# The sums of batches three and four by way of DRAM, and a first block in halves

## The chip, the cores and the metric

The kernel runs on one core of a Trainium2 chip. The metric is the device time of one execution in microseconds; a kernel's time is the median over several executions. The engines are named as the profile names them: PE (TensorE, matrix products), PEld (its weight loads), DVE (VectorE), ACT (ScalarE), POOL (GpSimd) and SP (SyncE, which here only issues transfers). Every engine works through its own list of instructions in order.

## The reference

A polynomial-sketch attention feeds a feed-forward layer. There are 4 batches, 4 heads, 1088 positions and 32 values per head; the sketch has r = 8, so a feature vector has 64 entries. All inputs and the output are float32.

```python
a = einsum('rd,bhsd->bhsr', S1, x);  b = einsum('rd,bhsd->bhsr', S2, x)
phi(x) = einsum('bhsi,bhsj->bhsij', a, b).reshape(..., 64)

kv  = einsum('bhsf,bhsd->bhfd', phi(k), v)      # sums of values, 64 x 32 a head
z   = sum(phi(k), axis=2)                       # own sums, 64 a head
num = einsum('bhsf,bhfd->bhsd', phi(q), kv)
den = einsum('bhsf,bhf->bhs', phi(q), z) + 1e-06
x   = (num / den), heads side by side           # 4352 x 128
out = maximum(x @ w_in, 0)**2 @ w_out           # w_in 128 x 2048, w_out 2048 x 128
```

## The kernel before

**The feed-forward layer as a stream of blocks.** The 4352 rows are cut into eight chunks of 512 (two of each batch, `ci = 2 * b + g`) and a ninth of 256 for the remainders. A chunk takes 16 blocks, one for each 128 columns of `w_in`. In a block PE multiplies `xT` (float16, rows along the free axis) by 128 columns of `w_in` into `pg` (L949), DVE or ACT takes the maximum with zero into `gt`, ACT or POOL squares it into `g`, and PE adds the product with 128 rows of `w_out` to `po` (L1037, float32, in two passes, hence "x2" in the profile). `block()` first calls `first_product()` until the stream holds more than `LOOK` = 3 finished first products, then takes the oldest for the second product. `now[0]` counts the blocks that were written out. After each block `pump` lets a number of generators ("lanes") write out some of the remaining work, so the order on every engine is fixed when the kernel is built; `dve_time`, `pool_time`, `quiet` and the like are the writer's guesses of how busy an engine is, used only for that.

**The attention of a batch** (`batch_gen`, for batches 1 to 3; batch 0 is written out by hand at the start). Blocks of `k` and `q` are turned by DVE, projected (L269, L288), and copied by ACT (L292, L294). The features of `q` are made by POOL (L338) from two factors, `f[0]` and `f[1]`, which `factors_gen` spreads over the partitions by way of DRAM: for each group `g` of a batch one transfer `q_one` and two `q_two` out (L311, L316), and two transfers `f` back (L325, L328). All of these are issued by SP, group 0 first and group 1 six blocks later. The features of `k` are made by POOL as outer products (L356).

`KvRows.products` then has PE form the sums of values, `kvr_ps` (L439; four heads of 32 rows each, 64 features along the free axis), and the own sums (L394). ACT copies both to SBUF (L458, L462). `spread` puts them into the block-diagonal matrix `kvbd[b]`, which has 128 partitions (two heads of 64 features) and, for two pairs of heads, 33 columns a head: 32 sums of values and the own sum. For that PE turns the sums of values with the identity (`turn`, L480) and picks the own sums with a 0/1 matrix (`pick_sums`, L406) into `kvt_ps`; ACT copies the values into place (`place`, L488), and DVE masks and adds up the own sums (`own_sums`, L414, L421).

Only then can `x_gen` write out the numerators and denominators of 512 rows (`nd`, L269, PE). `normalize` divides and scales on DVE and gives `xs`, whose turned form is the chunk's `xT`. There are two ways for that. If at the time of writing fewer than 15 blocks are left before the chunk's own first block (L626, `16 * chunk - now[0] < 15`), PE turns it with four transposes into `x_ps` (L631) and ACT copies it (L636). Otherwise DVE turns blocks of 32 (`xsT`, L648) and five transfers put them in place by way of DRAM (L650, L656). `second_gen` does the features and `x_gen` of a batch's second group, after the first group's chunk is there.

A finished chunk's `po` is turned by DVE (L917), scaled on POOL (L922) and stored by four transfers (L929). The scales go to all partitions by two small transfers (`beta`, L670, L671).

**SP's queue.** SP issues nearly all transfers in the order in which they were written out. An issue waits when its source is not ready, and everything behind it waits too.

**The start.** Batch 0 is written out by hand (L1046 to L1146). While the first rows are normalised, PE does products whose results nobody reads (`idle_products`). `first_two` then does the first products of blocks 0 and 1 at once: DVE and ACT each take one maximum, ACT and POOL one square each. The last two of four casts of `w_in` to float16 (L1143) follow on ACT before the stream begins. `later` lists loads by the block before which they are written out.

Of the kernel before, what the change touches and what calls it, by code (L numbers as in the profile page):

```python
# [21 lines left out]
def kernel(  # L22
# [17 lines left out]
    nc = tc.nc  # L40
# [198 lines left out]

    def idle_products(n, slow=False):  # L240
        idle_ps = pspool.tile([128, 512], F32, name="idle_ps", tag="po", bufs=2)
        for i in range(n):
            if slow:
                nc.tensor.matmul(idle_ps[:, :], zero_w[:, :], _v(zero_w, 0, [[0, 512]]))  # L244
            else:
                nc.tensor.matmul(idle_ps[:, :], zero[:, 0:128], zero[:, :])  # L246
# [181 lines left out]
    class KvRows:  # L428
# [34 lines left out]

        def products(self, phs):
            for g in range(2):
# [8 lines left out]
            self.rest_sums()  # L474
            self.keep_rows()
            self.keep_sums()

# [8 lines left out]
        def place(self, t_ps):  # L486
            for x in range(2):
                act.copy(  # L488
                    _v(kvbd[self.b], VW * x, [[2 * VW, 2], [1, D]], 64 * x, 64),
                    _v(t_ps, 0, [[D, 2], [1, D]], 64 * x, 64),  # L490
                )

        def spread(self):
# [268 lines left out]
    def batch_gen(b):  # L762
# [49 lines left out]
        kv = KvRows(b, ab_k)  # L812
        kv.products(phk)
        yield 1, 0
        nd_taken[0] = False
        yield from ms_both()
        ms_used()
        t_ps = kv.spread()
        yield 1, 0
        yield from dve_ready(1.0)  # L820
        own_sums(b, t_ps, 64)
        dve_time(0.6)
        lanes.append([second_gen(b, fs, w, phT, n1), n1 + 10, 0])
        yield 1, 0
        while not made_ph[b]:
# [3 lines left out]
    def second_gen(b, fs, w, phT, n1):  # L829
# [4 lines left out]
        for g in range(2):  # L834
            if w[g] > 512:
                u = b - 1 + g
                phT_rem[u] = [phT[g][pr][:, 512:576] for pr in range(2)]
                rests.append(u)
        yield 1, 0
        yield from x_gen(b, 1, phT[1], rests)  # L840
        if b % 2 == 1:
# [131 lines left out]

    def first_two():
        xT = chunks[0][0]
        pgs, gts, g2s = [], [], []
        for c in range(2):
            pgs.append(pspool.tile([128, 512], F32, name="pg", tag="pg", bufs=2))
            nc.tensor.matmul(pgs[c][:, :], w_in[:, 128 * c : 128 * c + 128], xT[:, :])
            gts.append(fpool.tile([128, 512], F32, name="gt", tag="gt", bufs=3))  # L980
            g2s.append(fpool.tile([128, 512], F32, name="g2", tag="g2", bufs=4))
        dve.tensor_scalar(
            out=gts[0][:, :], in0=pgs[0][:, :], scalar1=0.0, scalar2=None, op0=amax
        )
        act.activation(gts[1][:, :], pgs[1][:, :], Relu)
        act.activation(g2s[0][:, :], gts[0][:, :], Square)
        pool.tensor_tensor(out=g2s[1][:, :], in0=gts[1][:, :], in1=gts[1][:, :], op=mult)
        for c in range(2):
            stream.append((0, c, 512, g2s[c]))
            made[0] += 1  # L990

# [24 lines left out]
    def block():  # L1016
        while len(stream) <= LOOK and first_product():
            pass
# [4 lines left out]
        if nt < 512:  # L1023
# [7 lines left out]
            if c == NC - 1:  # L1031
                rows_store(0, ci)
                for args in held:
                    rows_product(*args)
                rows_store(1, ci)
            return
        nc.tensor.matmul(  # L1037
# [42 lines left out]
    outer(phq, pq[1], 0, 2, dve, pq[0])  # L1080
    outer(phq, pq[1], 3, 1, pool)
    for t in range(4):
        kv0.tile(phk[0], 0, t)
    zt_ps = pspool.tile([128, 32], F32, name="zt_ps", tag="po", bufs=2)
    pick_sums(zt_ps, 0, kv0.sums)
    outer(phq, pq[1], 2, 1, dve, pq[0])
# [5 lines left out]

    def turned_half(ph, t0, engs):
        t_ps = pspool.tile([128, 512], F32, name="t_ps", tag="ms", bufs=2)
        for pr in range(2):
            for t in (t0, t0 + 1):
                nc.tensor.transpose(  # L1097
                    _v(t_ps, 256 * pr + 128 * (t - t0), [[1, 128]]),
                    ph[:, 256 * t + 128 * pr : 256 * t + 128 * pr + 128],
                    iden[:, :],  # L1100
                )
        halves = []
# [26 lines left out]
    beta = next(norm)  # L1129
    idle_products(2)  # L1130
    chunk_of(0, 0, xT0, beta)
    for b in range(1, B):
        pool.memset(kvbd[b][:], 0.0)
        clear_rest(b)
    first_two()
    pq1 = proj(xq1, "ms")
    phq1 = ph_tile("ph_q", 2)
    for t0 in (0, 2):
        outer(phq1, pq1[1], t0, 2, pool)
    for _ in range(2):  # L1140
        first_product()
    for c in range(2, 4):
        act.copy(  # L1143
            w_in[:, 512 * c : 512 * c + 512], w_in32[:, 512 * c : 512 * c + 512]
        )
    nd_taken[0] = True  # L1146
# [15 lines left out]
    add_work(*(batch_gen(b) for b in range(1, B)))  # L1162
    later = []
    for b in range(2, B):
# [3 lines left out]
        later.append((n + 5, load_all, (q_sb[b], q, b)))  # L1168
        later += [(n + 6 + i, load_v_rest, (b, i, sp)) for i in range(2)]
    while len(stream) or made[0] < NC * (2 * B + 1):  # L1170
        while later and later[0][0] <= now[0]:
# [38 lines left out]
```

## Time and profile before

| What | Value |
|---|---|
| Median of 3 runs | 195.78 us (195.59 to 196.67) |
| Profiled execution, its own time | 195.83 us |
| Its span, first to last instruction | 194.0 us |
| PE, DVE, ACT, POOL busy | 186.3, 116.7, 109.2, 73.4 us |
| Second products L1037, x256 | 130.7 us |
| First products L949, x126 | 47.8 us |
| Features of `q` on POOL, L338 x12 | 16.1 us, idle before them 11.6 us for `f` |
| Idle products L246, x12 | 4.7 us |
| Transfers on SP's queue | 34400 packets, 22.27 MB |
| Mean granted clock of PE | 0.995 |

The span is that of one profiled execution, so sums of its parts are set against 194.0 us; some 1.8 us of the measured time lie outside it. Products are pipelined and overlap in the profile, so the chain that ended last, which counts every moment once, is a better price list for PE than mean durations. "Idle before, and what ended it" tells which other engine or transfer released an instruction. A row of SP is the time that the issue took, not the transfer itself.

### The profile page before, as it was taken

How to read it: one execution, taken by the hardware profiler on the slowest of the kernel's cores; microseconds unless marked ns; L12 is line 12 of the kernel's file. 1: busy time of each engine (PE TensorE's matmuls, PEld its weight loads, DVE VectorE, ACT ScalarE, POOL GpSimd, SP SyncE). 2: the span in 40 equal slices, each digit the busy share in tenths (PEclk: the TensorE clock that was granted, in tenths of full speed). 3: DMA queues.
4: the chain of work that ended last, by engine and by line, in shares of the span. 5: the costliest groups of instructions: out<-in, count | busy, mean ns of one | idle time of the engine just before them, and what ended most of it. 6: DMA issues, size and time to landing. Idle time of an engine off the chain costs nothing.

```text
span 194.0 us, 3759 instructions
## 1 busy us (share of the span) xinstructions
PE 186.3 (96%) x1390; PEld 97.0 (50%) x1390; DVE 116.7 (60%) x268; ACT 109.2 (56%) x215; POOL 73.4 (38%) x100
## 2 busy tenths in 40 slices
PE   7699999999999999999999999999899999999992
PEld 2573554545545454635454545454544344444791
DVE  4866785465477639376867264584477645544771
ACT  3254757654565964654847564557464665465470
POOL 4507502565247029251733280726124222522200
PEclk9999999999999999999999999999999999999998
DMA  5999674398953808974000467396011400300031
GB/s 160 268 314 228 159 216 132 66 234 203 233 203 93 198 4 198 275 219 84 4 3 0 81 164 199 80 222 144 3 25 33 63 7 0 54 0 0 9 51 27
DMA packets 34658, 22.58 MB, mean 116 GB/s; under 512 B 24720, under 2 KB 30096, under 8 KB 34640
## 3 DMA queue, kind: packets, MB, share of 16 engines
q1 hardware_dynamic: 34400, 22.27, 46.5%
q8 instruction: 11, 0.18, 0.4%
q10 hardware_dynamic: 240, 0.07, 0.2%
q14 instruction: 7, 0.06, 0.1%
HBM read 15.97 MB, written 6.37 MB: 115 GB/s over the span
## 4 chain that ended last, share of the span: by engine, by line
PE 85%; DVE 3%; issue 2%; DMA 2%; POOL 2%; SPq 2%; ACT 1%; POOLq 0%
PE po L1037 51%; PE pg L949 15%; PE nd L269 5%; PE kvr_ps L439 2%; DMA v_sb<-in_v_dram 2%; PE po L996 2%; PE po_r L996 2%; PE ab_ps L269 2%; POOL phF L338 1%; DVE gt L966 1%; PE ab_ps L288 1%; PE t_ps L1097 1%; PE idle_ps L244 1%; SPq L119 1%; PE kvt_ps L480 1%
## 5 line engine op out<-in xcount | busy, mean ns | idle before, releaser
L1037 PE MATMUL po<-g,w_o 128*128 128x512 f32 x256 | 130.7, 592 | 0.1
L966 DVE TENSOR_SCALAR gt<-pg 128x512 f32<-128x512 f32 (+1 forms) x105 | 67.7, 647 | 57.7 <-PE pg L949 49.9
L969 ACT ACTIVATE g<-gt 128x512 f32<-128x512 f32 (+1 forms) x105 | 62.6, 597 | 58.6 <-DVE gt L966 55.5
L1037 PEld LDWEIGHTS po<-g,w_o 128*128 128x128 f32 x256 | 48.5, 191 | 38.5 <-issue 20.1
L957 POOL TENSOR_TENSOR g<-gt 128x512 f32<-128x512 f32 x22 | 22.9, 1039 | 69.6 <-ACT gt L956 69.6
L949 PE MATMUL pg<-xT,w_in 128*128 128x512 f16 x126 | 47.8, 380 | 0.2 <-DVE gt L966 0.2
L949 PEld LDWEIGHTS <-w_in 128*128 128x128 f16 x142 | 13.8, 98 | 26.3 <-issue 25.3
L338 POOL TENSOR_TENSOR phF<-f,f 128x576 f32<-128x576 f32 (+1 forms) x12 | 16.1, 1361 | 11.6 <-DMA f<-q_two 11.6
L356 POOL TENSOR_TENSOR ph_k<-ab 128x512 f32<-128x512 f32 x14 | 14.5, 1070 | 10.4 <-ACT ab L294 9.0
L956 ACT ACTIVATE gt<-pg 128x512 f32<-128x512 f32 x22 | 12.8, 582 | 0.1
L922 POOL TENSOR_TENSOR o_sb<-oT,beta_t 128x512 f32<-128x512 f32 x8 | 8.4, 1048 | 5.2 <-DVE oT L917 4.9
L963 ACT ACTIVATE g<-gt 128x512 f32<-128x512 f32 x15 | 9.4, 629 | 0.6
L269 PEld LDWEIGHTS nd<-kvbd,phF 128*64 128x64 f32 x208 | 6.9, 137 | 5.3 <-issue 3.0
L962 ACT ACTIVATE gt<-pg 128x512 f32<-128x512 f32 x15 | 8.8, 585 | 0.0
L269 PE MATMUL nd<-kvbd,phF 128*64 128x66 f32 x208 | 7.9, 225 | 0.6 <-POOL phF L338 0.6
L917 DVE STREAM_TRANSPOSE oT<-po 128x512 f32<-128x512 f32 x8 | 5.7, 717 | 3.8 <-PE po L1037 3.5
L269 PEld LDWEIGHTS ab_ps<-w_bd,xt 128*64 128x64 f32 x160 | 6.1, 138 | 3.5 <-issue 1.4
L269 PE MATMUL ab_ps<-w_bd,xt 128*64 128x64 f32 x160 | 6.3, 224 | 1.1 <-DVE xt L257 1.1
L996 PE MATMUL po<-w_o,g 128*128 128x128 f32 x32 | 6.2, 278 | 0.0
L257 DVE STREAM_TRANSPOSE xt<-q_sb 128x512 f32<-128x512 f32 x8 | 5.4, 696 | 1.2 <-DMA q_sb<-in_q_dram 1.1
L996 PE MATMUL po_r<-w_o,g 128*128 128x128 f32 x32 | 6.0, 275 | 0.0
L246 PE MATMUL idle_ps<-zero 128*128 128x512 f16 x12 | 4.7, 522 | 1.3 <-DVE own L193 1.2
(131 smaller groups left out, 139.2 us busy)
## 6 DMA issues: line engine op xcount, KB each, us to landing
q_two<-qf SPq DMA_DIRECT2D x8, 288.0 KB
f<-q_one SPq DMA_DIRECT2D x4, 576.0 KB
f<-q_two SPq DMA_DIRECT2D x4, 576.0 KB
v_sb<-in_v_dram SPq DMA_DIRECT2D x16, 128.0 KB
out_dram<-o_sb SPq DMA_DIRECT2D x32, 64.0 KB
k_sb<-in_k_dram SPq DMA_DIRECT2D x3, 544.0 KB
q_sb<-in_q_dram SPq DMA_DIRECT2D x3, 544.0 KB
w_in<-in_moe_w_in_dram SPq DMA_DIRECT2D x2, 512.0 KB
```

What stands on the lines that cost most here:

```text
L269: nc.tensor.matmul(out_ps[p0 + c : p0 + c + z, c0 : c0 + w], lhsT[:, l0 + c : l0 + c + z], rhs)
L338: pool.tensor_tensor(out=ph[:, c], in0=fs[g][0][:, c], in1=fs[g][1][:, c], op=mult)
L356: eng.tensor_tensor(out=_v(ph, 256 * t0, [[64, 4 * m], [8, 8], [1, 8]]), in0=_v(ab if a is None else a, c0, [[n, 4 * m], [1, 8], [0, 8]]), ...
L949: nc.tensor.matmul(pg[:, 0:nt], w_in[:, 128 * c : 128 * c + 128], xT[:, 0:nt])
L956: act.activation(gt[:, 0:nt], pg[:, 0:nt], Relu)
L957: pool.tensor_tensor(out=g2[:, 0:nt], in0=gt[:, 0:nt], in1=gt[:, 0:nt], op=mult)
L962: act.activation(gt[:, 0:nt], pg[:, 0:nt], Relu)
L963: act.activation(g2[:, 0:nt], gt[:, 0:nt], Square)
L966: dve.tensor_scalar(out=gt[:, 0:nt], in0=pg[:, 0:nt], scalar1=0.0, scalar2=None, op0=amax)
L969: act.activation(g2[:, 0:nt], gt[:, 0:nt], Square)
L996: nc.tensor.matmul(po[r][:, 0:128], g2[:, 128 * r : 128 * r + 128], w_o[:, 128 * c : 128 * c + 128], start=c == 0, stop=c == NC - 1,)
L1037: nc.tensor.matmul(po[0][:, 0:nt], w_o[:, 128 * c : 128 * c + 128], g2[:, 0:nt], start=(c == 0), stop=(c == NC - 1),)
```

## The change

It has four parts.

1. For batches 2 and 3 (the third and fourth), `spread` and `own_sums` are replaced by `by_dram`. ACT copies the own sums and DVE turns the sums of values in blocks of 32 x 32, both into one tile `kept`. SP writes them to DRAM in two transfers and reads them back in eight: two of `kvbd` and two of `zs` for each half of the partitions. DVE adds up the four candidates of each own sum straight into `kvbd`. `second_gen` is added as a lane before that instead of after it, and now waits for POOL's counter before its `x_gen`. Batch 1 stays with `spread`.
2. The first block is done in two halves of 256 rows (`in_halves`), the first on DVE alone, the second on ACT alone; its second product has two halves too. The first blocks look ahead by `now[0] + 1` instead of 3.
3. At the start `pick_sums` comes before the first sums of rows, one idle product of two goes, and the casts of the second half of `w_in` are written out after blocks 3 and 6.
4. `turned_half` gets an argument `z` that nobody sets.

As L626 depends on the block counter, the way in which a chunk is turned can change with it.

```diff
...
@@ -461,7 +461,7 @@
             self.sums = apool.tile([128, 32], F32, name="kvz", tag="kvz")
             act.copy(self.sums[:, :], self.sums_ps[:, 0:32])
 
-        def products(self, phs):
+        def products(self, phs, keep=True):
             for g in range(2):
                 for t in range(4):
                     self.tile(phs[g], g, t)
@@ -472,8 +472,9 @@
                         self.sums_ps, self.abs, 128 * g + 32 * t, 256, t, g == 0, g == 1 and t > 0
                     )
             self.rest_sums()
-            self.keep_rows()
-            self.keep_sums()
+            if keep:
+                self.keep_rows()
+                self.keep_sums()
 
         def turn(self, t_ps):
             for x in range(2):
@@ -489,6 +490,54 @@
                     _v(kvbd[self.b], VW * x, [[2 * VW, 2], [1, D]], 64 * x, 64),
                     _v(t_ps, 0, [[D, 2], [1, D]], 64 * x, 64),
                 )
+
+        def by_dram(self):
+
+
+            b = self.b
+            kept = apool.tile([128, 96], F32, name="kept", tag="kept")
+            act.copy(kept[:, 64:96], self.sums_ps[:, 0:32])
+            dve.transpose(kept[:, 0:64], self.ps[:, 0:64])
+            parts = dpool.tile([128, 64], F32, name=f"kept{b}", tag=f"kept{b}")
+
+            kz = dpool.tile([32, 128], F32, name=f"keptz{b}", tag=f"keptz{b}")
+            sp.dma_start(parts[:, :], kept[:, 0:64])
+            sp.dma_start(
+                bass.AP(kz.tensor, kz.offset, [[8, 128], [1024, 4], [1, 8]]),
+                _v(kept, 64, [[8, 4], [1, 8]]),
+            )
+            yield 3, 0
+            zs = apool.tile([128, 8], F32, name="zs", tag="zs")
+            for x in range(2):
+                for i in range(2):
+                    sp.dma_start(
+                        _v(
+                            kvbd[b], VW * x, [[2 * VW, 2], [1, D]], 64 * x + 32 * i, 32
+                        ),
+                        bass.AP(
+                            parts.tensor, parts.offset + 32 * 64 * x + 32 * i,
+                            [[64, 32], [64 * 64, 2], [1, 32]],
+                        ),
+                    )
+                for pr in range(2):
+                    sp.dma_start(
+                        _v(zs, 4 * pr, [[1, 4]], 64 * x, 64),
+                        bass.AP(
+                            kz.tensor, kz.offset + (1024 + 64) * (2 * pr + x),
+                            [[1, 64], [256, 4]],
+                        ),
+                    )
+                yield 1, 0
+            yield 2, 0
+            yield from dve_ready(1.0)
+            for x in range(2):
+                dve.tensor_reduce(
+                    out=_v(kvbd[b], VW * x + D, [[2 * VW, 2]], 64 * x, 64),
+                    in_=_v(zs, 0, [[4, 2], [1, 4]], 64 * x, 64),
+                    axis=AX,
+                    op=add,
+                )
+            dve_time(0.4)
 
         def spread(self):
             t_ps = pspool.tile([128, 512], F32, name="kvt_ps", tag="ms", bufs=2)
@@ -810,17 +859,26 @@
             yield 1, 0
         yield from take_nd()
         kv = KvRows(b, ab_k)
-        kv.products(phk)
-        yield 1, 0
-        nd_taken[0] = False
-        yield from ms_both()
-        ms_used()
-        t_ps = kv.spread()
-        yield 1, 0
-        yield from dve_ready(1.0)
-        own_sums(b, t_ps, 64)
-        dve_time(0.6)
+        if b > 1:
+            yield from dve_ready(1.0)
+        kv.products(phk, b == 1)
         lanes.append([second_gen(b, fs, w, phT, n1), n1 + 10, 0])
+        if b == 1:
+            yield 1, 0
+            nd_taken[0] = False
+            yield from ms_both()
+            ms_used()
+            t_ps = kv.spread()
+            yield 1, 0
+            yield from dve_ready(1.0)
+            own_sums(b, t_ps, 64)
+            dve_time(0.6)
+        else:
+            moved = kv.by_dram()
+            dve_time(0.4)
+            yield next(moved)
+            nd_taken[0] = False
+            yield from moved
         yield 1, 0
         while not made_ph[b]:
             yield 1, 0
@@ -836,7 +894,10 @@
                 u = b - 1 + g
                 phT_rem[u] = [phT[g][pr][:, 512:576] for pr in range(2)]
                 rests.append(u)
+        ready = pool_free[0]
         yield 1, 0
+        while now[0] < ready and not hurry[0]:
+            yield 1, 0
         yield from x_gen(b, 1, phT[1], rests)
         if b % 2 == 1:
             add_work(rest_x(b // 2))
@@ -971,23 +1032,31 @@
         made[0] += 1
         return True
 
-    def first_two():
+    def half(t, i):
+
+        return _v(t, 64 * i, [[128, 4], [1, 64]])
+
+    def in_halves(c):
+
         xT = chunks[0][0]
-        pgs, gts, g2s = [], [], []
-        for c in range(2):
-            pgs.append(pspool.tile([128, 512], F32, name="pg", tag="pg", bufs=2))
-            nc.tensor.matmul(pgs[c][:, :], w_in[:, 128 * c : 128 * c + 128], xT[:, :])
-            gts.append(fpool.tile([128, 512], F32, name="gt", tag="gt", bufs=3))
-            g2s.append(fpool.tile([128, 512], F32, name="g2", tag="g2", bufs=4))
+        pgs, gts, g2s = [
+            [tl.tile([128, 512], F32, name=n, tag=n, bufs=bufs) for i in range(2)]
+            for tl, n, bufs in ((pspool, "pg", 2), (fpool, "gt", 3), (fpool, "g2", 4))
+        ]
+        for i in range(2):
+            nc.tensor.matmul(
+                pgs[i][:, 0:256], w_in[:, 128 * c : 128 * c + 128], half(xT, i)
+            )
         dve.tensor_scalar(
-            out=gts[0][:, :], in0=pgs[0][:, :], scalar1=0.0, scalar2=None, op0=amax
-        )
-        act.activation(gts[1][:, :], pgs[1][:, :], Relu)
-        act.activation(g2s[0][:, :], gts[0][:, :], Square)
-        pool.tensor_tensor(out=g2s[1][:, :], in0=gts[1][:, :], in1=gts[1][:, :], op=mult)
-        for c in range(2):
-            stream.append((0, c, 512, g2s[c]))
-            made[0] += 1
+            out=gts[0][:, 0:256], in0=pgs[0][:, 0:256], scalar1=0.0, scalar2=None, op0=amax
+        )
+        act.activation(gts[1][:, 0:256], pgs[1][:, 0:256], Relu)
+        dve.tensor_tensor(
+            out=g2s[0][:, 0:256], in0=gts[0][:, 0:256], in1=gts[0][:, 0:256], op=mult
+        )
+        act.activation(g2s[1][:, 0:256], gts[1][:, 0:256], Square)
+        stream.append((0, c, 512, g2s))
+        made[0] += 1
 
     po = [None, None]
     held = []
@@ -1014,7 +1083,7 @@
             (sp, act)[i].dma_start(dst, _v(o_sb, 0, [[1, 128]], 64 * i, 64))
 
     def block():
-        while len(stream) <= LOOK and first_product():
+        while len(stream) <= min(LOOK, now[0] + 1) and first_product():
             pass
         ci, c, nt, g2 = stream.pop(0)
         if c == 0:
@@ -1033,6 +1102,13 @@
                 for args in held:
                     rows_product(*args)
                 rows_store(1, ci)
+            return
+        if ci == 0 and c == 0:
+            for i in range(2):
+                nc.tensor.matmul(
+                    half(po[0], i), w_o[:, 128 * c : 128 * c + 128], g2[i][:, 0:256],
+                    start=(c == 0 and i == 0), stop=False,
+                )
             return
         nc.tensor.matmul(
             po[0][:, 0:nt], w_o[:, 128 * c : 128 * c + 128], g2[:, 0:nt],
@@ -1079,10 +1155,10 @@
     kv0.keep_sums()
     outer(phq, pq[1], 0, 2, dve, pq[0])
     outer(phq, pq[1], 3, 1, pool)
+    zt_ps = pspool.tile([128, 32], F32, name="zt_ps", tag="po", bufs=2)
+    pick_sums(zt_ps, 0, kv0.sums)
     for t in range(4):
         kv0.tile(phk[0], 0, t)
-    zt_ps = pspool.tile([128, 32], F32, name="zt_ps", tag="po", bufs=2)
-    pick_sums(zt_ps, 0, kv0.sums)
     outer(phq, pq[1], 2, 1, dve, pq[0])
     own_sums(0, zt_ps, 0)
     kv0.rest()
...
@@ -1127,22 +1205,18 @@
     norm = normalize_first(nd0, xT0)
     next(norm)
     beta = next(norm)
-    idle_products(2)
+    idle_products(1, tag="ms")
     chunk_of(0, 0, xT0, beta)
     for b in range(1, B):
         pool.memset(kvbd[b][:], 0.0)
         clear_rest(b)
-    first_two()
+    in_halves(0)
     pq1 = proj(xq1, "ms")
+    first_product()
+    block()
     phq1 = ph_tile("ph_q", 2)
     for t0 in (0, 2):
         outer(phq1, pq1[1], t0, 2, pool)
-    for _ in range(2):
-        first_product()
-    for c in range(2, 4):
-        act.copy(
-            w_in[:, 512 * c : 512 * c + 512], w_in32[:, 512 * c : 512 * c + 512]
-        )
     nd_taken[0] = True
 
 
@@ -1160,13 +1234,17 @@
 
     lanes.append([second_group(), 2, 1])
     add_work(*(batch_gen(b) for b in range(1, B)))
-    later = []
+    def cast(c):
+        act.copy(w_in[:, 512 * c : 512 * c + 512], w_in32[:, 512 * c : 512 * c + 512])
+
+    later = [(3, cast, (2,)), (6, cast, (3,))]
     for b in range(2, B):
         n = (2, 27)[b - 2]
         later.append((n, load_all, (k_sb[b], k, b)))
         later += [(n + 1 + h, load_v, (b, h)) for h in range(H)]
         later.append((n + 5, load_all, (q_sb[b], q, b)))
         later += [(n + 6 + i, load_v_rest, (b, i, sp)) for i in range(2)]
+    later.sort(key=lambda x: x[0])
     while len(stream) or made[0] < NC * (2 * B + 1):
         while later and later[0][0] <= now[0]:
             _, what, args = later.pop(0)
```

## The prediction

> **What bounds the kernel now.** I read the table of busy time first, then the chain that ended last, then the queue of SP between 70 and 100 us, then the start and the end in order of time. The first line of the page says which engine counts.
>
> ```profile
> PE 186.3 (96%) x1390; PEld 97.0 (50%) x1390; DVE 116.7 (60%) x268; ACT 109.2 (56%) x215; POOL 73.4 (38%) x100
> ```
>
> PE is busy 186.3 of 194.0 us, and the chain that ended last runs through PE for 85% of the span. So a removed PE instruction is worth its length, and a wait at the head of PE's queue costs its length; work elsewhere counts only when PE waits for it. The chain, in order of time, around the sums of batch 2 (the "batch three" of the change):
>
> ```profile
> 79.15 1.14 PE kvr_ps L439 x72
> ...
> 80.78 0.86 PE po L1037 x2
> 81.64 0.27 PE kvt_ps L480 x4
> 81.91 0.19 PE kvt_ps L406 x8
> 82.10 0.32 PE pg L949
> 82.42 0.86 PE po L1037 x2
> ...
> 87.58 1.09 PE nd L269 x32
> ```
>
> Between two products at L1037 lie 1.64 us where the turn stands (82.42 - 80.78); the ordinary distance in the same chain is 1.075 us (0.22 + 0.86). I call one such 1.075 us step a block and count blocks by the products at L1037: the sums `kvr` come after block 45, the numerators `nd` after block 51.
>
> SP's own queue over the same time (start, length, line, transfer):
>
> ```profile
> 72.13 0.50 SPq L311 DMA_DIRECT2D q_one<-qf  x1
> ...
> 77.31 0.35 SPq L328 DMA_DIRECT2D f<-q_two  x1
> 77.71 0.47 SPq L311 DMA_DIRECT2D q_one<-qf  x1
> 78.24 1.23 SPq L316 DMA_DIRECT2D q_two<-qf  x2
> 81.31 0.54 SPq L325 DMA_DIRECT2D f<-q_one  x1
> 84.96 0.34 SPq L328 DMA_DIRECT2D f<-q_two  x1
> 88.02 1.98 SPq L929 DMA_DIRECT2D out_dram<-o_sb  x4
> 94.79 0.58 SPq L670 DMA_DIRECT2D beta<-beta  x1
> 96.77 0.56 SPq L671 DMA_DIRECT2D beta_t<-beta  x1
> ```
>
> Two things are to be seen. SP issues in order, and the transfer `f<-q_two` of the second group waits until 84.96 for `q_two` to land, though the sums `kvr` are done at 80.46. And a small write that is read back costs 1.98 us from the start of the one issue to the start of the other (94.79 to 96.77).
>
> **The change, part by part.**
>
> *The turn leaves PE (gain).* Two spreads (L480, L406) go: 2 x (1.64 - 1.075) = -1.13 us. ACT loses two copies per batch and DVE three short instructions for one 128x64 transpose (L263, 0.22) and two reductions (0.18 each, L421): off PE's path.
>
> *Chunks 5 and 7 turned by PE again (loss).* L626 chooses by the block counter. The sums now return later, so in the changed kernel's instruction lists both chunks take the branch with four `x_ps` transposes instead of the trip by DRAM. The chain prices four at 0.22 us (68.11, L631): 2 x 0.22 = +0.43 us. DVE saves two `xsT` (0.70 each).
>
> *The start (gain).* `pick_sums` moves ahead of the sums of rows, which wait for `v_sb` until 8.91. The copy it needs (L462) ends at 8.61, so 0.34 us of PE go mostly under that wait: -0.25. One idle product of two goes ahead of the first `pg`: -0.22. Then:
>
> ```profile
> 16.78 0.59 PE L979 MATMUL pg<-xT,w_in 128*128 128x512 f16 x2
> ...
> 18.60 1.13 PE L1037 MATMUL po<-g,w_o 128*128 128x512 f32 x2
> ```
>
> From first `pg` to first `po` 1.82 us pass now. In halves: 0.31 to the first half's result (17.20 - 16.78, less half a `pg` of 0.22), 0.42 (gt 128x256 at L966, mean of 16), 0.40 (128x256 tensor_tensor, L356), 0.05 signal: 1.18 us. ACT's half, 0.42 + 0.42, is ready before the second half is called. But two of the four `pg` that PE now does inside that stretch (0.43) come after it in the new order, so of 0.64 us I keep 0.21. Start together: -0.7 (between -0.4 and -1.0). The casts of `w_in` (L1143) only move to later gaps of ACT, 3.05 of 5 us busy at 25 to 30 us; if ACT were full there, 1.1 us would show.
>
> *Two waits that go.* PE waits once in the middle for features on POOL:
>
> ```profile
> 136.69 1.27 PE L269 MATMUL nd<-kvbd,phF 128*64 128x66 f32 x32 [0.60 <-POOL phF L338]
> ```
>
> In the new order `nd` of that group comes after block 94 instead of 88 and `second_gen` waits for POOL's counter: -0.6. Near 149 to 153 us three blocks take 0.6 us more than 3 x 1.075, as DVE does the remainder's norms between its `gt`; without `xsT` I take half: -0.3 (0 to -0.6).
>
> Gains in sum: -0.7 - 1.13 + 0.43 - 0.6 - 0.3 = -2.3 us.
>
> *The trip of the sums by DRAM (the step that decides).* Per batch SP gets two writes and eight reads, and in SP's list they stand behind all five transfers of the second group, the last of them `f<-q_two`. The `nd` after block 54 (batch 2) waits for them, and nothing is behind it on PE that may pass. DVE holds too, at the reduction of `zs`; the two `gt` behind it are needed only after `nd`.
>
> Batch 2: `f<-q_two` is issued by 85.30 - 0.7 = 84.6. The writes follow at once, but its own data fill the DMA engines until 87.9 - 0.7 = 87.2 (DMA share in half-microsecond windows: 1.02 at 87.0, 0.37 at 87.5, 0.02 at 88.0), so I let the writes land at 88.0; on free engines it would be 84.6 + 2.0 = 86.6. Then in SP's order: two reads of `kvbd` and two of `zs` (0.5 each), the four stores of `o_sb` (1.98, row 88.02), four reads (2.0), and 1.5 us from the end of the last issue to its landing (1.98 less 0.5): 88.0 + 2.0 + 2.0 + 2.0 + 1.5 = 95.5, and two reductions, 0.4: 95.9. PE is there at 87.58 - 0.7 - 0.57 + 3 x 1.075 = 89.5. Stall: 6.4 us.
>
> Batch 3, counted from its first issue of `q_one` (t): `f<-q_two` is out at t + 13.2 (85.30 - 72.13), the writes land at t + 16.6, eight reads in a row without stores between, 4.0, landing 1.5, reductions 0.4: t + 22.5. PE reaches `kvr` at t + 7.0 (79.15 - 72.13), and with 1.31 us for `kvr`, 0.1 for the switch and nine blocks the `nd` after block 85 at t + 18.1. Stall: 4.4 us.
>
> No row shows these very reads. Lower end: the writes land 2.0 us after issue, each issue 0.43 (L119): stalls of 4.4 and 2.5. Upper end: 0.98 per issue (the longest of L656): 10.3 and 8.4. I stay with 0.5: the medians of the nearest rows, the small transfers at L929, L656, L671 and L670, are 0.49, 0.53, 0.55 and 0.56. If the cover were whole, the price would be zero; if none, it would be all of the trip from `kvr` on, over 14 us.
>
> *The clock.* The windows after PE's last product, at 190.24:
>
> ```profile
> 191.00:192.00 1.00, 0.00 (x0) 0.00 (x0) 0.00 (x0) 0.00 (x0) 0.00 (x0) 1.00 0.28 66
> 192.00:193.00 1.00, 0.00 (x0) 0.00 (x0) 0.00 (x0) 0.00 (x0) 0.00 (x0) 0.62 0.28 66
> 193.00:194.00 1.00, 0.00 (x0) 0.00 (x0) 0.00 (x0) 0.00 (x0) 0.00 (x0) 0.50 0.00 0
> ```
>
> The seventh number is the granted clock: it falls to half 2.0 us after PE stops. Both stalls are longer. How long it stays low once PE works again no row shows; between nothing and twice the fall, and I take the 2.0 us of the fall itself: at half speed that loses 1.0 us, twice: +2.0 (0 to 4). [...] The trace agrees on the half rate (0.50) and shows no return.
>
> **Sum.** 194.0 - 2.3 + 6.4 + 4.4 + 2.0 = 204.5 us of span. Outside the span the profiled execution has 195.83 - 194.0 = 1.8 us: 206.3. It lies 0.05 above the median of 195.78, so nothing is corrected.
>
> **The rivals.**
>
> *The trip fits (faster).* For it: on an empty queue the write-and-read costs some 2 + 2 us, and the change leaves nine blocks, 9.7 us. It decides from the point where SP could issue the writes about 6 us earlier, near 80 us, with the reads not queued behind the stores. Against it: SP's list and the row at 84.96. Time: 195.8 - 2.3 = 193.5 if no stall is left. Chance 0.12, 0.09 of it faster and 0.03 with one or two us of stall left.
>
> *Short stalls, clock unharmed.* Writes overtake `f`'s data and issues take 0.43: 195.8 - 2.3 + 4.4 + 2.5 = 200.4. For it: the shares of the DMA engines are under 1 in places. Against: the rows of the same window with 2.6 and 3.0 us from beta write to read when rings are full (119.87, 131.75). Chance 0.16.
>
> *The clock stays low longer.* PE works at half speed for twice the time of the fall, 4 us after each stall, and loses 2.0 us each instead of 1.0: 206.3 + 2.0 = 208.3. For it: the rows stay at 0.50 for the last 1.8 us. Against: PE stands still in those, and the second stall may be too short for a full fall. [...] Chance 0.24.
>
> **How the numbers follow.** The forecast has 0.48, with 206.3. Slower in three cases: 0.48 + 0.16 + 0.24 = 0.88. From 0.5% on (1 us) a measurement of this kernel can tell a change. The range: below 199 lies the case that fits; the bounds of the sum are 195.8 - 2.9 + 6.9 = 199.8 and 195.8 - 1.7 + 18.7 + 4 = 216.8 (gains of 2.9 and 1.7 at their ends), the latter only with all ten issues and the clock at their worst. I take 199 to 212. The likeliest case's own range is 202.5 to 210.
>
> **What would show it.** In the changed profile PE waits at L269 for `nd` twice, about 6 and 4 us, released by a DMA read of `kvbd` or by DVE's reduction of `zs`; SP issues the writes of the sums right behind `f<-q_two`, some 4 us after `kvr`; the clock's row falls there. No `kvt_ps` in batches 2 and 3, eight more `x_ps` transposes, first `po` near 17.5 us. The prediction is wrong if PE passes both `nd` without a wait of over 1 us, or if the writes stand ahead of the second group's transfers in time.

## The result and the profile after

The changed kernel takes 211.29 us (median of 4 runs, 210.29 to 211.92); the kernel before, on the same chip, 196.12 us (4 runs, 195.59 to 196.67). The ratio is 1.077, with a 95% interval of 1.071 to 1.082. Medians in this document are over all executions of a kernel, ratios over those within 1.5% of its fastest, as an execution now and then takes longer at a lower clock (one of e10's six 196.59 us at a mean of 0.982). The profiled execution took 211.34 us, with a span of 209.5 us. Line numbers from here on are those of the kernel that is shown: in the changed kernel the second product is L1113 (L1037 before), the first product L1010, the writes of the sums L504 and L505, their reads L513 and L523, DVE's reduction of `zs` L534.

The head of the page after, with PE's busy time, the clock that PE was granted (in 40 slices, tenths) and the chain by engine:

```profile
PE 190.2 (91%) x1376; PEld 100.5 (48%) x1376; DVE 117.2 (56%) x269; ACT 108.5 (52%) x210; POOL 73.6 (35%) x100
PEclk9999999999999999975799999996699999999998
PE 75%; DMA 13%; SPq 7%; DVE 1%; issue 1%; ACT 1%; DVEq 0%
```

PE's share fell from 96% to 91%, the clock has two holes, and a fifth of the chain is now transfers (13%) and SP's queue (7%). PE's list of waits names the two places (total, times, longest):

```profile
PE nd L269 <- DVE kvbd L534: 8.0, 1, 8.0
PE nd L269 <- DMA out_dram<-o_sb: 5.5, 1, 5.5
```

The first is batch 2. The second is batch 3; it carries another transfer's name only because that was the last thing to land before PE went on (issued at 143.50, landed at 145.50). PE needed the reduction of `zs` there as well: it ends at 145.41, and `nd` starts at 145.51.

```profile
145.25 0.16 DVE L534 TENSOR_REDUCE kvbd<-zs 64x2 f32<-64x8 f32 x1 [2.25 <-DMA zs<-keptz]
```

The chain of batch 2 in order of time:

```profile
78.58 1.14 PE kvr_ps L439 x72
...
82.36 0.87 PE po L1113 x2
83.26 0.73 DVE oT L978
84.02 4.77 DMA kept<-kept
88.85 0.32 SPq L513
...
94.96 2.36 DMA zs<-keptz
...
97.42 0.17 DVE kvbd L534
...
97.68 2.03 PE nd L269 x32
99.71 0.54 PE pg L1010
100.25 1.71 PE po L1113 x2
```

And SP's queue over the same time:

```profile
83.63 0.34 SPq L328 DMA_DIRECT2D f<-q_two  x1
84.02 0.43 SPq L504 DMA_DIRECT2D kept<-kept  x1
84.55 0.38 SPq L505 DMA_DIRECT2D keptz<-kept  x1
88.85 0.79 SPq L513 DMA_DIRECT2D kvbd<-kept  x2
89.69 1.30 SPq L523 DMA_DIRECT2D zs<-keptz  x2
91.09 2.18 SPq L990 DMA_DIRECT2D out_dram<-o_sb  x4
93.32 0.97 SPq L513 DMA_DIRECT2D kvbd<-kept  x2
94.34 1.24 SPq L523 DMA_DIRECT2D zs<-keptz  x2
```

The writes stand right behind `f<-q_two`, 4.1 us after PE finished the sums (79.89). The first read can be issued 4.83 us after the first write (88.85 - 84.02), the four stores of a finished chunk stand in the middle of the reads, and PE, which stopped at 89.66, starts at 97.68. When it does, `nd` takes 2.03 us where 1.09 us is usual and a pair of second products 1.71 us instead of 0.86: the clock is at 0.50. One-microsecond windows (the seventh number is the granted clock):

```profile
91.00:92.00 1.00, 0.00 (x0) 0.00 (x0) 0.00 (x0) 0.00 (x0) 0.00 (x0) 1.00 0.18 1
92.00:93.00 1.00, 0.00 (x0) 0.00 (x0) 0.12 (x1) 0.00 (x0) 0.00 (x0) 0.56 0.73 102
...
101.00:102.00 1.00, 1.00 (x3) 0.30 (x2) 0.93 (x4) 0.63 (x1) 0.00 (x0) 0.50 0.00 0
102.00:103.00 1.00, 1.00 (x3) 0.47 (x3) 0.80 (x5) 0.52 (x1) 0.00 (x0) 0.82 0.00 0
103.00:104.00 1.00, 1.00 (x4) 0.48 (x3) 0.38 (x1) 0.71 (x2) 0.00 (x0) 1.00 0.00 0
```

A window in which the clock changes gives the moment: 0.56 is full clock for 0.12 of the window and half for the rest, so it fell at 92.12; 0.82 puts the return at 102.36. From the restart of `nd` to the third `po` after it PE needed 5.83 us (103.51 - 97.68) for what takes 3.57 us at full clock (1.09 + 0.32 + 2 x 0.86 + 2 x 0.22): 2.26 us lost. Batch 3 looks the same: the clock is low from 143.32 to 150.15 and 2.24 us are lost.

With that the whole span is accounted for: 194.0 + 13.5 (two waits) + 4.5 (clock) - 2.5 = 209.5. The 2.5 us are not measured; they are what the sum leaves for the gains.

### The profile page after: what moved, and what is told of

Same layout as the page of the kernel before. It is cut to its first block, busy times and chain, and to the rows that moved or that the text cites. A ratio compares the mean times of both kernels' runs of the same rounds, so it can differ in the third digit from the quotient of the medians.

```text
span 209.5 us, 3743 instructions
## 1 busy us (share of the span) xinstructions
PE 190.2 (91%) x1376; PEld 100.5 (48%) x1376; DVE 117.2 (56%) x269; ACT 108.5 (52%) x210; POOL 73.6 (35%) x100
## 4 chain that ended last, share of the span: by engine, by line
PE 75%; DMA 13%; SPq 7%; DVE 1%; issue 1%; ACT 1%; DVEq 0%
PE po L1113 44%; PE pg L1010 13%; PE nd L269 5%; DMA kept<-kept 5%; DMA q_two<-qf 4%; PE ab_ps L269 2%; SPq L523 2%; DMA q_sb<-in_q_dram 2%; PE po L1065 2%; PE po_r L1065 2%; SPq L513 2%; PE kvr_ps L439 2%; PE ab_ps L288 1%; DMA zs<-keptz 1%; SPq L990 1%
## 5 line engine op out<-in xcount | busy, mean ns | idle before, releaser
L1113 PE MATMUL po<-g,w_o 128*128 128x512 f32 x254 | 131.6, 601 | 0.1
L1030 ACT ACTIVATE g<-gt 128x512 f32<-128x512 f32 (+1 forms) x107 | 63.8, 598 | 75.0 <-DVE gt L1027 72.5
L1027 DVE TENSOR_SCALAR gt<-pg 128x512 f32<-128x512 f32 (+1 forms) x107 | 69.0, 648 | 54.2 <-PE pg L1010 48.1
L1113 PEld LDWEIGHTS po<-g,w_o 128*128 128x128 f32 x254 | 49.1, 194 | 38.7 <-issue 17.7
L1018 POOL TENSOR_TENSOR g<-gt 128x512 f32<-128x512 f32 x23 | 24.0, 1041 | 76.9 <-ACT gt L1017 76.8
L1010 PE MATMUL pg<-xT,w_in 128*128 128x512 f16 x127 | 48.9, 388 | 0.0
L1010 PEld LDWEIGHTS <-w_in 128*128 128x128 f16 x143 | 14.1, 99 | 26.8 <-issue 25.5
L269 PE MATMUL nd<-kvbd,phF 128*64 128x66 f32 x208 | 9.4, 254 | 13.5 <-DVE kvbd L534 8.0
L338 POOL TENSOR_TENSOR phF<-f,f 128x576 f32<-128x576 f32 (+1 forms) x12 | 16.1, 1365 | 11.7 <-DMA f<-q_two 11.7
L269 PEld LDWEIGHTS nd<-kvbd,phF 128*64 128x64 f32 x208 | 8.5, 165 | 18.2 <-issue 18.2
L1017 ACT ACTIVATE gt<-pg 128x512 f32<-128x512 f32 x23 | 13.4, 581 | 0.0
L534 DVE TENSOR_REDUCE kvbd<-zs 64x2 f32<-64x8 f32 x4 | 0.6, 157 | 17.1 <-DMA zs<-keptz 17.1
L1023 ACT ACTIVATE gt<-pg 128x512 f32<-128x512 f32 x13 | 7.6, 588 | 1.7 <-PE pg L1010 1.7
L1024 ACT ACTIVATE g<-gt 128x512 f32<-128x512 f32 x13 | 8.2, 630 | 0.4
```

The lines of the kernel that those rows point to most:

```text
L269: nc.tensor.matmul(out_ps[p0 + c : p0 + c + z, c0 : c0 + w], lhsT[:, l0 + c : l0 + c + z], rhs)
L338: pool.tensor_tensor(out=ph[:, c], in0=fs[g][0][:, c], in1=fs[g][1][:, c], op=mult)
L1010: nc.tensor.matmul(pg[:, 0:nt], w_in[:, 128 * c : 128 * c + 128], xT[:, 0:nt])
L1017: act.activation(gt[:, 0:nt], pg[:, 0:nt], Relu)
L1018: pool.tensor_tensor(out=g2[:, 0:nt], in0=gt[:, 0:nt], in1=gt[:, 0:nt], op=mult)
L1024: act.activation(g2[:, 0:nt], gt[:, 0:nt], Square)
```

## The experiments

Theory: SP's order holds the sums' trip back (the writes stand behind the second group's transfers, the reads behind each other and behind the stores), and the stalls cost clock on top. Rivals: the trip is slow wherever it stands; the stalls alone cost it, the clock nothing; the rest of the change brings less than it seems. The kernel before ran beside all of them and its median was 196.50 to 196.68 us.

### e1: the start alone

Only the start of the change is kept; the sums of all batches are turned by PE as before.

```diff
-        if b > 1:
-            yield from dve_ready(1.0)
-        kv.products(phk, b == 1)
+        kv.products(phk)
...
+        t_ps = kv.spread()
```

> The changed start (pick_sums first, one idle product less, first block in halves, casts later) with the sums of every batch put in place by PE, ACT and DVE as before. My theory: the start is worth what the chains of the two profiles differ by, 79.15 - 78.58 = 0.57 us, and nothing else changes: 195.5 us against 196.1 before. Rival: the gain at the start is given back later, as the stream then runs into the same waits earlier (0.6 us for phF, 0.6 us near 150 us): 196.1. A second rival, that the start costs something which the stalls of the changed kernel hid: over 196.5.

Measured: 197.02 us (12 runs), ratio 1.003 (1.000 to 1.006). So the start alone gains nothing that can be measured; it is not what made the kernel slower either. Its profile shows the sums of batch 2 at 78.89, where before has 79.15 and the changed kernel 78.58, and those 0.26 us are gone by the `nd` of batch 3 (136.91 against 136.69): the chain there has a wait for DVE's `gt` at 121.59 that before has not.

### e2: the clock kept up

The changed kernel, with products that nobody reads ahead of the two numerators that wait. They lie in the stall and keep PE busy; all else is as in the changed kernel.

```diff
+            if b > 1 and g == 0:
+                idle_products((0, 0, 36, 24)[b], tag="ms")
             nd = numerators(b, phT)
```

> The changed kernel with 36 and 24 products that nobody reads (0.22 us each, 7.8 and 5.2 us) ahead of the two nd that wait for kvbd, where PE stands still for 8.0 and 5.5 us. My theory: a stall costs its length and then 2.25 us more, as PE works at half the clock for some 4.5 us after it; with PE kept busy the clock stays at 1.00, the waits end at the same time, and 211.3 - 4.5 = 206.8 us are left. Rival: what follows the stall is slow for another reason (engines that refill their buffers): the clock's row stays up but the time stays at 211.

Measured: 207.70 us, ratio 1.057 (1.053 to 1.061): 3.6 us less than the changed kernel, with the transfers as they were. The granted clock over the span is 1.00, and of the two stalls a wait of 0.9 us is left, in batch 3:

```profile
PE nd L269 <- issue: 0.9, 1, 0.9
```

So some 3.6 us of the 15 us loss are clock alone, most of the 4.5 us read from the windows. In batch 2 the products that nobody reads last until 97.89, 0.7 us beyond DVE's last reduction (97.16), so e2 adds an estimated 0.6 us of its own; that brings the two figures closer still.

### e3: the second group's transfers behind the reads

```diff
             fs.append(f)
-            yield 6, 0
+            yield 6 if b == 1 else 13, 0
```

> The changed kernel with the second group's five transfers (q_one, two q_two, two f) put behind the reads of the sums on SP's queue in batches 2 and 3; PE's, DVE's and ACT's order is unchanged. My theory: the stalls come from the place in SP's queue. Batch 2's writes go out near 80.5 instead of 84.0 us, but the four stores of o_sb still lie between its reads and wait for POOL until 86.4: reads end near 90.9, landing 1.8, so some 3 us of the 8.0 us stall are left; batch 3 has no stores between and its stall of 5.5 us goes. 211.3 - 4.8 - 5.5 and 2.2 to 4.5 us of clock: 196.5 to 198.8 us. Rival: the write itself is slow (32-byte pieces, 4.8 us from issue to the reads, as in the profile): batch 2 keeps 4 to 5 us and batch 3 about 1 us: 200 us or more.

Measured: 199.62 us, ratio 1.015 (1.011 to 1.019); 11.7 us of the 15.2 us are gone, though the number of transfers and their sizes are unchanged, and PE, DVE, ACT and POOL carry out the same instructions in the same order in both traces. (The same holds for e4, e8 and e10.) Batch 3 no longer waits for the sums, batch 2 still does, as the stores still stand between the reads:

```profile
PE nd L269 <- DVE kvbd L534: 3.2, 1, 3.2
```

### e4: and all eight reads in a row

e3, and in `by_dram` the reads issued one behind the other:

```diff
-                yield 1, 0
-            yield 2, 0
+            yield 4, 0
```

> As the kernel before in this call, and all eight reads of the sums in a row, with the stores behind them. My theory: batch 2's writes go out near 80.5, land in 2.2 us as nothing is ahead of them, eight reads take 4.2, landing 1.8 and the reduction 0.3: 89.0 us, before PE is there at 89.7: no stall over 0.5 us, clock at 1.00, 211.3 - 13.5 - 4.5 = 193.3 us, faster than the kernel before the change. Rival: the write takes 4.8 us by itself: kvbd is ready at 91.6, 2 us of stall in batch 2 and about 0.5 in batch 3, 196 us or more.

Measured: 197.30 us (10 runs), ratio 1.003 (1.000 to 1.006). SP's queue of e4:

```profile
80.97 0.34 SPq L504 DMA_DIRECT2D kept<-kept  x1
...
82.48 0.79 SPq L513 DMA_DIRECT2D kvbd<-kept  x2
...
87.13 2.17 SPq L989 DMA_DIRECT2D out_dram<-o_sb  x4
...
94.74 0.35 SPq L328 DMA_DIRECT2D f<-q_two  x1
```

The wait of `nd` for the sums is gone. The first read is out 1.51 us after the first write, not 4.83: the write itself is not slow, and the rival "the trip is slow wherever it stands" falls. But the forecast of 193.3 us does not come either. The second group's `f<-q_two` is now issued at 94.74 instead of 84.96 in the kernel before, and the wait for what POOL makes of it, 0.6 us before, has grown:

```profile
PE nd L269 <- POOL phF L338: 1.3, 2, 1.0
```

### e5, e6, e7: the second group's stores early, its loads late

To have `f` sooner, e5 issues the three stores of the second group behind those of the first and keeps only its two loads behind the sums' reads. e6 also puts `pick_sums` back to where it was at the start, e7 the whole start of before.

```diff
+        first, second = store(0), store(1)
+        load(*first)
+        yield 13, 0
+        load(*second)
```

> e4 with the second group's three stores (q_one, q_two) issued right behind the first group's, ahead of the sums, and only its two loads of f behind the sums' reads. Theory (what e4 still pays is a late second phF: its f landed at 99.8 in batch 2 and the numerators began at 102.75): the second f<-q_two is issued near 89.5 and lands near 93.5, the waits PE nd <- POOL phF (1.3 us in e4) go, 196.0 us, ratio to before 0.995 to 1.000. Rival (the second group's stores now lie in the rings ahead of the sums' writes and slow them as the loads did in the changed kernel): the sums come 1 to 3 us late, a wait PE nd <- DVE kvbd is back, 197.5 to 200 us.

> e5 with the start's pick_sums put back behind the four kv0.tile, as in the kernel before. Theory (in the new order the matmuls of kvr wait for ACT's kvz: PE zt_ps <- ACT kvz 0.4 us in e1 and e4): that wait goes and the first second product starts 0.2 to 0.4 us sooner than in e5; 195.7 us, ratio to e5 0.998. Rival (q's load ends the start either way): no difference from e5.

> e5 with the whole start of the kernel before (first block in one piece, sums picked where they were, casts at once): the DRAM trip in its better place alone. If the start is worth the 0.57 us that the changed kernel's profile showed, this is 0.5 to 0.6 us above e5. Rival (e1's 1.0027 [0.9997, 1.0058] says that the start gains nothing): the same as e5 or up to 0.5 us below it.

Measured: e5 197.97 us, ratio 1.008 (1.005 to 1.010); e6 198.13, 1.006 (1.003 to 1.009); e7 198.70, 1.010 (1.006 to 1.015). The rival was right: the sums come late, and `nd` waits for them again. A line of e5's chain, one of PE's waits and two of SP's queue:

```profile
78.29 6.24 DMA f<-q_two
```

```profile
PE po L1123 <- POOL g L1028: 1.9, 2, 1.5
```

```profile
81.67 0.34 SPq L515 DMA_DIRECT2D kept<-kept  x1
...
85.94 0.79 SPq L524 DMA_DIRECT2D kvbd<-kept  x2
```

The first group's `f` lands 6.24 us after its issue, POOL is late with features and then with a square that PE waits for, and the write comes back after 4.27 us instead of the 1.51 us of e4. The busy share of the transfer engines from 80 to 84 us is 0.98 to 1.03 in e5 and 0.09 to 0.27 in e4. `nd` of batch 2 starts at 92.68, 0.1 us after DVE's last reduction of `zs` (92.41 + 0.16). That wait of 1.2 us stands under "issue" in e5's list of waits; e6's list has 1.3 us under `DVE kvbd`. The three intervals overlap, so e6 and e7 tell nothing apart.

### e8: the reads in a row, the writes where the change has them

The changed kernel with e4's edit of `by_dram` alone.

> The changed kernel with only the eight reads of the sums issued in a row, ahead of the output's stores; the second group's five transfers stay ahead of the writes. Theory (of the 8.0 us of batch 2 some 2.8 are the stores of 2.2 us and the blocks between the reads, the rest the queue place of the writes; each stall over 3 us costs 2.2 us of clock whatever its length): waits of PE nd <- DVE kvbd of 5.2 and 4.6 us, clock loss unchanged, 207.6 us. Rival (stores and blocks between the reads are the whole delay): waits under 1.5 us and no clock loss, 197 to 199 us.

Measured: 209.18 us, ratio 1.061 (1.054 to 1.069). The waits of `nd` are 4.74 us in batch 2 and 5.42 us in batch 3 (expected 5.2 and 4.6), and the clock falls twice as in the changed kernel:

```profile
94.81 2.03 PE L269 MATMUL nd<-kvbd,phF 128*64 128x66 f32 x32 [4.74 <-DMA out_dram<-o_sb]
142.35 2.03 PE L269 MATMUL nd<-kvbd,phF 128*64 128x66 f32 x32 [5.42 <-DMA out_dram<-o_sb]
```

Batch 2 lost 3.3 us of its 8.0 us stall: 2.2 us are the stores that no longer stand among the reads, and in this execution the reads began 0.7 us sooner (88.11) and PE came 0.4 us later (90.07). Batch 3 had no stores there and keeps its stall (5.5 us in the changed kernel). What is left is the place of the writes: e4, which differs from e8 only in having the second group's transfers behind the reads, has no such wait.

### e9: the writes on ACT's queue

e8 with both writes issued by ACT, so that they need not wait for `f<-q_two` in SP's order.

```diff
-            sp.dma_start(parts[:, :], kept[:, 0:64])
-            sp.dma_start(
+            act.dma_start(parts[:, :], kept[:, 0:64])
+            act.dma_start(
```

> e8 with the two writes (kept, keptz) issued by ACT instead of SP, so that they no longer stand behind f<-q_two in SP's order; reads, second group and everything else as in e8. Theory (most of the stall is the writes' place in SP's order: 3.0 us of waiting for the second group's q_two, and then f's data ahead of them in the rings): the writes go out near 81, land near 83, the reads follow f<-q_two at once (84.4 instead of 88.1), the wait of batch 2 falls from 5.4 to 1.5 us, that of batch 3 from 4.8 to 1, the clock stays up: 195.7 to 197.5 us. Rival (the second group's data in the rings slows the small transfers wherever they are issued): the reads still begin after 87 and wait and clock loss stay, 205 to 209 us.

Measured: 204.65 us (6 runs, 201.23 to 206.93), ratio 1.028 (1.024 to 1.033), which by the kernel before beside it is 202.1 us, between theory and rival. (The expectation has the two waits of e8 the wrong way round.) The writes are issued at 82.83, but by the chain they return 3.28 us later, and the reads, still behind `f<-q_two` on SP, start only at 87.40. PE waits 3.9 us in batch 2 and 1.3 us in batch 3. The chain of e9:

```profile
82.83 3.28 DMA kept<-kept
...
95.98 2.03 PE nd L269 x32
```

So a queue of its own took away the waiting in order, but the write itself stayed slow, 3.28 us for the 1.51 us of e4: the transfer engines' busy share is 0.86 to 1.02 from 80 to 84 us, when the second group's data are under way (0.09 to 0.27 in e4). The reads need a place as well. SP issued the second group's `f<-q_one` only at 86.18, 6.8 us after `q_one` (79.37; in the changed kernel's execution 3.6 us, 77.12 to 80.75). SP's list of waits puts 5.0 us of that down to the landing of the very write that ACT had issued:

```profile
SPq L325 <- DMA kept<-kept: 5.0, 1, 5.0
```

In batch 3 `f<-q_two` likewise goes out at 132.83, just after that write landed (132.75). The two transfers share no tile, and why one should wait for the other was not settled. So e9 does not show what the writes on a free queue would be worth.

### e10, e11, e12: the second group right behind the reads

e10 is e4 with the second group's five transfers between the reads and the stores of the finished chunk, 2.2 us of issues sooner. e11 is e10 with the start of the kernel before; e12 is e10 with only `pick_sums` put back.

```diff
+            for _ in more:
+                pass
             yield 4, 0
...
-            moved = kv.by_dram()
+            moved = kv.by_dram(factors_gen(b, qf, w, fs, (1,)))
```

> e4 with the second group's five transfers between the sums' reads and the output's stores, 2.2 us sooner than in e4. Theory (what e4 still pays over the kernel before is the second phF, late by 1.0 and 0.3 us): f<-q_two lands near 97.6 instead of 99.8, the wait PE nd <- POOL phF is under 0.3 us, and with the eight shorter spreads 195.8 us, ratio to before 0.995 to 1.000. Rival (e4's 1.2 us over before come from elsewhere, or the stores of the output are now late for o_sb): no better than e4, 197.3 us, 1.003.

> e10 with the start of the kernel before (first block in one piece, sums picked behind the four kv0.tile, casts at once). If the gain of e10 (196.50 to 194.26) is all of the shorter spreads, this is the same as e10, ratio 0.986 to 0.993. If the start is worth the 0.57 us that the changed kernel's profile showed, it is 0.991 to 0.995. If the start is what gains, it is 1.00.

> e10 with only pick_sums put back behind the four kv0.tile. Theory (q's load and v's load end the start either way, as e6 against e5 showed): the same as e10, ratio to before 0.986 to 0.993. Rival (the wait for kvz of 0.4 us is on the path): 0.3 to 0.4 us below e10, 0.984 to 0.991.

Measured: e10 194.26 us, ratio 0.989 (0.986 to 0.992); e11 194.43, 0.990 (0.986 to 0.993); e12 194.46, 0.991 (0.988 to 0.994). All three beat the kernel before, by 2.1 to 2.2 us of median, and the three cannot be told apart: the whole gain is in the batches, and the start is worth nothing here. SP's queue of e11:

```profile
81.94 0.34 SPq L504 DMA_DIRECT2D kept<-kept  x1
82.33 0.49 SPq L505 DMA_DIRECT2D keptz<-kept  x1
83.56 0.79 SPq L513 DMA_DIRECT2D kvbd<-kept  x2
...
86.87 1.24 SPq L523 DMA_DIRECT2D zs<-keptz  x2
88.15 0.61 SPq L311 DMA_DIRECT2D q_one<-qf  x1
...
93.63 0.34 SPq L328 DMA_DIRECT2D f<-q_two  x1
94.06 2.28 SPq L991 DMA_DIRECT2D out_dram<-o_sb  x4
```

The reads are out by 88.1, `nd` starts at 91.17 right behind a block, and of the stores nothing waits. The lists of PE's waits of e10 and e11 have three entries each, all at the start of the kernel. From the sums of batch 2 to those of batch 3 e11 needs 40.05 us for 31 blocks, before 39.32 us for 30: less one block of 1.075, that is 0.35 us gained. From there to the last product it needs 68.96 us, before 71.78 us with one block more: 1.75 us gained.

## Why the prediction was right, and where it was off

**The deciding step** was right. Both waits are where it put them, behind the releaser it named, with SP's list as the cause: e3 and e4 move nothing but places in that list and the time falls from 211.3 to 197.3 us. The smaller signs came too: 29 `x_ps` transposes instead of 21, no `kvt_ps` in batches 2 and 3, the first `po` at 17.28. The time is another matter: 211.3 us is 5.0 us above the forecast of 206.3, outside the likeliest case's own 202.5 to 210 and only 0.7 us inside the range. The next two terms make up that difference: 2.7 + 2.5, less 0.2 us of gains.

**The size of the stalls** (6.4 and 4.4 us; measured 8.0 and 5.5) is a term that was too small by 2.7 us. Batch 2 by its parts: the reads begin at 88.85 instead of 88.0 (+0.85; the writes come back after 4.8 us instead of 3.4); the last issue starts at 94.96 instead of 93.5 (+0.6 more, as a read of `zs` takes over 0.6 and not 0.5 us and the four stores 2.2 and not 2.0 us); from there to DVE 2.46 us instead of 2.0 (+0.46); the reductions 0.26 us instead of 0.4 (-0.14); PE arrives at 89.66 instead of 89.5 (-0.16). The sum is 1.6 us. In batch 3 the reads were late by only 0.3 us (t + 16.9 for t + 16.6), the rest again issues and landing. Two readings beside the sum were loose: the upper end of the stalls is 10.2 and 8.2 us by its own terms (10.3 and 8.4 are given), and the rows at 119.87 and 131.75 stand beside batch 3's sums and not in batch 2's window; the transfer engines are busy 0.86 to 1.19 over the second of them, but 0.28 to 0.34 from 120 to 122 us, behind the first.

**The clock** (2.0 us; measured 4.5) is the other term that was too small. The prediction let the clock stay low as long after the restart as the fall had taken, 2.0 us. It returned 4.7 and 4.6 us after. The rival that gave it 4 us was nearer in this term, and still low; its time of 208.3 us fell short because of the stalls. The last section sets beside each other where the returns stood.

**The gains** (2.3 us) have the right sum (2.5 us left over in the changed kernel, 2.1 us of median in e11) by luck, as the places are wrong. Batch 2 gives 0.35 us, just what the prediction's pieces give for one batch (0.565 for the turn less 0.215 for four transposes). Batch 3 gives that, the 0.6 us of the wait for POOL, and 0.8 us more. Of this 0.6 us are the blocks where DVE was late near 149 to 153, which follow each other without a wait in e11 (the prediction took half of it, 0.3 us). The start gives nothing: that step failed. The changed kernel's profile seemed to confirm it, with the sums of batch 2 0.57 us sooner, but its own load of `q_sb` took 4.05 us, and 4.35 to 5.06 us in other executions with the same start; there the gain is 0.26 us at most (e1), 0.04 us in e4, and none in some. With `pick_sums` first, PE's start hangs on that load, while in the start of before it hangs on `v_sb` (4.55 to 5.52 us). Both scatter over about 1 us, so the reordering swaps a wait for one load for a wait for the other; that e10, e11 and e12 take the same time agrees with this.

**The rivals.** "Short stalls, clock unharmed" fell with the waits above 5 us. "The trip fits" is what e10 to e12 are: with the writes out at 81.7 to 83.0 us (the rival said near 80) and the reads not behind the stores, which was the rival's condition, the result is 194.3 to 194.5 us, where the rival said 193.5.

What stays open: of the 3.0 us between e4 and e10 the two profiles show 1.9 us (from the sums of batch 2 to those of batch 3, 41.48 against 40.05 us, and 0.5 us after), with the late features as the named part; the rest is between executions. For e5 to e7 the links were read from the traces, and no run tests them one by one. What held SP back in e9 is open.

## What to carry to other kernels

Before moving work from an engine to a chain of small transfers, read the list of the queue they will stand in: the trip here took 1.5 us from the first write to the first read in one place (e4) and 4.8 us in another (the changed kernel), and the same change is 8% slower or 1% faster by that alone. Put a chain that something waits for ahead of large transfers that are needed later, and then price what those lose. A gain at the very start that one profile shows must be set against how far the loads of other executions scatter (here that of `q_sb`, 4.05 to 5.06 us).

## What was not expected of the hardware

In these executions the moments at which the granted clock changes lie whole steps of about 3.41 us apart. The shortest distance is that of e9, from a fall at 9.84 to a return at 13.25: 3.41 us. In the changed kernel the clock falls at 92.12, returns at 102.36, falls at 143.32 and returns at 150.15: the distances are 10.24, 40.96 and 6.83 us, within 0.05 us 3, 12 and 2 such steps. The next changes of e9, at 95.17 and 102.00, are 81.92 and 6.83 us on, within 0.1 us 24 and 2 steps. In e3 a wait of 3.2 us that ended at 93.58 let the clock fall at 94.57, a microsecond after PE was at work again, for one step; waits of 1.0 to 1.3 us in the batches (e4, e5, e9) left it at 1.00. Around the stalls the trace shows this: in the 3.41 us ahead of the fall at 92.12 PE was busy 0.95 us, some 28% of the time; in e9 PE was at work again at 95.98, 0.8 us after the fall at 95.17, and one step after that fall (98.59) the clock was still at 0.50; and in these four stalls the return stood at the end of the first step in which PE was busy throughout, 4.4 us after the restart in e3, 4.7 and 4.6 us in the changed kernel and 6.0 us in e9. What sets the steps no run shows. Of the low time after the restart half is lost (2.26 of 4.68 us and 2.24 of 4.64 us in the changed kernel), so these stalls, 3.2 to 8.0 us long, cost 1.7 to 3.0 us of clock each (for e3 and e9 an estimate, half of 3.41 and of 6.02 us), and the longest did not cost the most: 8.0 us cost 2.3 us of clock, 3.9 us (e9) cost 3.0. That the place of a stall among the steps counts for more than its length is the author's estimate from these four; no run varies the place alone.

The same happened at the start of some executions: in the profiled ones of e9 and e10 the load of `q_sb` took 4.94 and 5.06 us, PE waited for what DVE made of it (1.2 and 1.0 us), and the clock was low from 9.84 and from 10.46 for one step each. With both, their sums of batch 2 come 1.8 and 1.9 us later than those of the kernel before, and e10's profiled execution (195.79 us) is above its own median.
